# Attention and feed-forward on one core: dummy matmuls ahead of all, alternating row halves for the turned scores, row maxima as two bfloat16 parts

## The chip, the core and the metric

The kernel runs on one core of a Trainium2 chip. The metric is the device time in microseconds (us) of one execution. The kernel before takes 789.25 us (median of 3 runs, 789.15 to 789.5). The engines are named as in the profile: PE is the matmul engine TensorE (PEld its weight loads), DVE the vector engine, ACT the scalar engine, POOL GpSimd, SP the engine that issues nearly all transfers (DMA).

## The reference

An attention over keys and values pooled 8 to 1, then a layer norm and a feed-forward with a residual. The output must be this:

```python
k_p = k.reshape(B, H, Sp, pool, D).mean(axis=3)          # B = H = 8, S = 576, D = 64, Sp = 72
v_p = v.reshape(B, H, Sp, pool, D).mean(axis=3)
scores = scale * np.matmul(q, k_p.transpose(0, 1, 3, 2))
scores = scores - np.max(scores, axis=-1, keepdims=True)
attn = np.exp(scores)
attn = attn / (np.sum(attn, axis=-1, keepdims=True) + 1e-09)
x = np.matmul(attn, v_p)                                 # heads side by side: (B, S, 512)
xn = (x - mu) / np.sqrt(var + 1e-06) * g_ln
out = x + np.maximum(xn @ w_ch1, 0.0) @ w_ch2            # 512 -> 2048 -> 512
```

## The kernel before

The 4608 tokens are 36 tiles `t` of 128 tokens, four to a chunk `c` of 512. The attention of a tile is `scores(t)` (PE, then row maxima `mx` on DVE), the exponentials, and `values(t)` (PE, then the layer norm's sums on DVE). The feed-forward of a chunk is `ffn_in` and `ffn_out` (L1116, L1319) for the first two chunks and a seven-product scheme (`product`, L1160, and `out_seven`, L1277) for the rest. Both weight matrices are split into high and low float16 parts on the chip: `convert` (ACT L535 and L539, DVE L527 and L543) puts a float32 together out of the loaded halves, and `split_w` (ACT L483, then DVE L490 for W1; ACT L483 and L485, then POOL L487 for W2) splits it. Block b's parts lie where block b-1's float32 was, so that the split of b waits for the split of b-1.

The first chunk is special. The exponentials of tiles 0 to 3 are made turned, with the keys on the partitions. `scores(t)` leaves the tile's queries and `mx` in `E[t]`. `probs_turned(t, i)`, with i = 0 for the even heads and i = 1 for the odd ones, multiplies the pooled keys with the queries once more, four heads into one PSUM tile `ps_f` (L849, rows 0 to 63 of the array for i = 0 and rows 64 to 127 for i = 1), and then adds the negative row maxima to the same four results by four float32 matmuls against a negative identity `minus` (L854). ACT takes the exponential (L864) and its float16 part (L865), POOL the remainder (L867). There are three buffers of `ps_f` in this stage, and one of `ps_m`.

The order of all steps is a table of tokens written by hand. `START` covers the first chunks, `STEADY` the rest; a token calls the next step of a generator, so that the order of the tokens is the order on every engine. `LN.2` loads the tokens of batch 0's values, `V0` pools them by five float32 matmuls against a band matrix (L723), `K0` sums the first keys (DVE L1389), `A.t` is the scores of tile t, `E.t.i` the turned exponentials, `B.t` the values, `C.m.b` the conversion and `S.m.b` the split of a weight block, `M1.0` the maximum over W1's first half, `F` and `G` the feed-forward. Engines take their instructions in that order and wait where an input is missing. For `A.t`, DVE reduces the maxima at L800. `M1.0` issues eight dummy matmuls (L463) and the third turned layer norm twelve (L877), each 512 columns of the bfloat16 identity `ident` with no reader.

Of the kernel before, what the change touches and what calls it, by code (L numbers as in the profile page):

```python
# [8 lines left out]
F32 = mybir.dt.float32  # L9
F16 = mybir.dt.float16  # L10
BF16 = mybir.dt.bfloat16
# [3 lines left out]
ALU = mybir.AluOpType  # L15
# [3 lines left out]
P = 128  # L19
B, H, S, D = 8, 8, 576, 64  # L20
POOL = 8
KV = S // POOL
# [6 lines left out]
CH = 512  # L29
# [4 lines left out]
NKT = DM // P  # L34
NFT = FF // P
NPAIR = H // 2
# [21 lines left out]
WARM_MAX = 8  # L58
MAXM = {1: "dve", 2: "act"}
# [5 lines left out]
LN.2 LN.2 LK.0 LK.1 Q.0 K0 R.1.0 Q.1 R.1.1 R.1.2 R.1.3 A.0 Q.1 R.1.3 K0 LK.0 V0 R.1.2 A.0 A.0 A.0 LK.1 HV.1.0 LG R.1.1  # L65
# [309 lines left out]
def attn_ffn_kernel(ctx: ExitStack, tc: tile.TileContext, qT, kT, v, kvn, kvt, g, w1, w2, out):  # L375
    nc = tc.nc
# [103 lines left out]

    def split(src, scale, hi, lo, pool=False):

        nc.scalar.activation(out=hi, in_=src, func=AF.Copy, scale=scale)  # L483
        if pool:
            nc.scalar.activation(out=src, in_=src, func=AF.Copy, scale=scale)  # L485
            yield
            nc.gpsimd.tensor_tensor(out=lo, in0=src, in1=hi, op=ALU.subtract)  # L487
            return
        yield
        nc.vector.scalar_tensor_tensor(  # L490
            out=lo, in0=src, scalar=scale, in1=hi, op0=ALU.mult, op1=ALU.subtract
        )
# [268 lines left out]
    q_sb, E, PT, X, Z, zTs = {}, {}, {}, {}, {}, {}  # L761
# [19 lines left out]
    def scores(t):  # L781
# [19 lines left out]
        if t < TPC:  # L801
            E[t] = q, mx
            return
# [35 lines left out]
    def probs_turned(t, i):  # L839
        q, mx = E[t]  # L840
        mx = mx.rearrange("p a h -> p (a h)")
        if t not in PT:
            PT[t] = wk2.tile([P, 2 * H, P], F16, name="pt")
        pt = PT[t]
        et = phl[t % 2].rearrange("p a h k -> p (a h k)").bitcast(F32).rearrange("p (h c) -> p h c", h=H)
        ps = psum["ps_f"].tile([P, CH], F32, name="ps_f")[:KV].rearrange("p (h c) -> p h c", c=P)
        d = slice(i * D, (i + 1) * D)
        for n in range(NPAIR):
            nc.tensor.matmul(  # L849
                ps[:, n], lhsT=kblk[0][d, n, :], rhs=q[d, n], start=n == 0, stop=False, skip_group_check=True  # L850
            )
        for n in range(NPAIR):
            s = NPAIR * i + n
            nc.tensor.matmul(  # L854
                ps[:, n],
                lhsT=mx[:, s : s + 1].broadcast_to([P, KV]),
                rhs=minus,
                start=False,
                stop=n == NPAIR - 1,
                skip_group_check=True,  # L860
            )
# [531 lines left out]
    def in_tile(c, f, h=None):  # L1393
# [3 lines left out]
        "LK": load_first_k, "LG": load_g, "Q": load_q, "K0": first_k, "V0": lambda: pool_tokens_v(0), "LN": load_tokens, "D": spread_v,  # L1397
# [65 lines left out]
```

## Time and profile before

| | |
|---|---|
| median of 3 runs | 789.25 us |
| span of the profiled execution | 789.2 us |
| PE busy | 772.6 us (98%) |
| PEld busy | 593.2 us (75%) |
| DVE busy | 626.3 us (79%) |
| ACT busy | 469.6 us (60%) |
| POOL busy | 486.9 us (62%) |

The span is the profiled execution's own time; times in rows count from its start. In a row of the timeline stand the start, the time from the start of the first to the end of the last instruction of a group, and in brackets how long the engine had been idle before it and who released it. Instructions overlap in their last part, so that the distance of two starts says what an instruction costs the next one. A float32 matmul stands in the records as two passes: "x8" is four matmuls.

### The profile page before, as it was taken

What the parts mean: (1) busy time and instruction counts of PE and PEld (TensorE: products, weight loads), DVE (VectorE), ACT (ScalarE), POOL (GpSimd) and SP (SyncE); (2) the same over time, 40 slices, a digit from 0 to 9 for tenths busy, and PEclk for the clock granted to TensorE, in tenths of its full rate; (3) what the DMA queues carried; (4) which work ended last, traced back from release to release, by engine and by line L of the source; (5) the groups of instructions that cost most, each with busy time, mean ns of one, the idle gap of its engine ahead of it and who ended that gap; (6) DMA issues with size and microseconds to landing.
All of it is one profiled execution on the core that took longest, in us unless ns stands there. A gap on an engine that the chain in (4) does not pass through costs nothing.

```text
span 789.2 us, 18979 instructions
## 1 busy us (share of the span) xinstructions
PE 772.6 (98%) x7458; PEld 593.2 (75%) x7458; DVE 626.3 (79%) x1296; ACT 469.6 (60%) x880; POOL 486.9 (62%) x597
## 2 busy tenths in 40 slices
PE   6999999999999999999999999999999999999998
PEld 3777444444458665788888888888888888888887
DVE  4998977787669898988789889996797768876554
ACT  3999883233316545577567665756576568555551
POOL 1786468746357766867645683776367638573553
PEclk9999999999999999999999999999999999999999
DMA  8968964631257788968867969578748666664243
GB/s 352 297 208 228 225 166 106 173 98 44 49 135 164 168 201 189 235 180 228 199 172 204 229 163 268 132 219 189 230 83 209 171 165 161 174 148 147 72 130 134
DMA packets 181513, 139.01 MB, mean 176 GB/s; under 512 B 143792, under 2 KB 151600, under 8 KB 179248
## 3 DMA queue, kind: packets, MB, share of 16 engines
q1 hardware_dynamic: 180272, 136.91, 65.2%
q8 instruction: 58, 0.95, 0.5%
q10 hardware_dynamic: 1152, 0.90, 0.4%
q14 instruction: 31, 0.25, 0.1%
HBM read 89.13 MB, written 16.78 MB: 134 GB/s over the span
## 4 chain that ended last, share of the span: by engine, by line
PE 81%; DVE 6%; ACT 6%; POOL 3%; DMA 2%; issue 1%; SPq 0%; POOLq 0%; DVEq 0%; ACTq 0%
PE ps_f L1160 29%; PE ps_f L1277 25%; PE ps_f L1319 14%; PE ps_f L1116 8%; PE ps_a L790 2%; PE ps_a L932 1%; DMA zts<-hl 1%; PE ps_a L933 1%; PE ps_m L723 1%; DVE w L1198 1%; POOL w L487 1%; DVE x L1294 1%; DMA w<-in_kvn_dram 1%; DMA ring<-w2s 1%; ACT w L483 1%
## 5 line engine op out<-in xcount | busy, mean ns | idle before, releaser
L1277 PE MATMUL ps_f<-ring,w 128*128 128x256 f16 x2016 | 231.8, 273 | 1.1 <-DVE x L1294 0.5
L1277 PEld LDWEIGHTS <-w 128*128 128x128 f16 x2016 | 196.1, 98 | 25.6 <-issue 2.0
L1160 PE MATMUL ps_f<-zts,w 128*128 128x256 f16 x1680 | 207.2, 273 | 0.4 <-ACT raw L1179 0.2
L1160 PEld LDWEIGHTS <-w 128*128 128x128 f16 x1680 | 162.9, 98 | 20.4 <-issue 0.8
L1319 PE MATMUL ps_f<-w,ring 128*128 128x512 f16 x576 | 126.8, 379 | 1.3 <-POOL w L487 1.3
L1319 PEld LDWEIGHTS <-ring 128*128 128x128 f16 x576 | 55.9, 98 | 67.1 <-issue 1.6
L1179 ACT COPY raw<-ps_f 128x256 f32<-128x256 f32 x160 | 56.0, 372 | 79.7 <-PE ps_f L1160 69.4
L1160 PE MATMUL ps_f<-zts,tsp 128*128 128x256 f16 x672 | 92.4, 273 | 1.3 <-ACT raw L1179 1.3
L1116 PE MATMUL ps_f<-zts,w 128*128 128x512 f16 (+1 forms) x480 | 85.9, 336 | 1.0 <-DVE ring L1127 1.0
L1196 ACT CAST w<-w 128x512 f16<-128x512 f32 x96 | 59.1, 619 | 38.2 <-POOL w L1219 20.3
L1198 POOL TENSOR_TENSOR w<-w 128x512 f16<-128x512 f32 x48 | 56.8, 1184 | 30.9 <-ACT w L1196 30.8
L1116 PEld LDWEIGHTS <-w 128*128 128x128 f16 x480 | 46.1, 98 | 36.6 <-issue 1.9
L1160 PEld LDWEIGHTS <-tsp 128*128 128x128 f16 x672 | 64.4, 98 | 10.2 <-issue 1.9
L1294 DVE SCALAR_TENSOR_TENSOR x<-ps_f,y,x 128x256 f32<-128x256 f32 (+1 forms) x84 | 42.3, 517 | 34.4 <-PE ps_f L1277 33.5
L826 POOL TENSOR_TENSOR phl<-e,phl 128x512 f16<-128x512 f32 x32 | 39.3, 1227 | 42.4 <-ACT phl L816 34.4
L1215 POOL TENSOR_TENSOR w<-raw 128x256 f32<-128x256 f32 x32 | 24.6, 768 | 56.4 <-ACT raw L1207 38.1
L1085 POOL TENSOR_TENSOR hl<-raw,hl 128x640 f16<-128x640 f32 x28 | 41.9, 1500 | 22.3 <-ACT hl L1083 22.3
L1294 DVE SCALAR_TENSOR_TENSOR x<-ps_f,cy,x 128x256 f32<-128x256 f32 (+1 forms) x84 | 42.2, 515 | 12.8 <-PE ps_f L1277 11.3
L1198 DVE TENSOR_TENSOR w<-raw,w 128x512 f16<-128x512 f32 (+1 forms) x64 | 44.6, 701 | 4.5 <-ACT w L1196 4.2
L1179 ACT COPY phl<-ps_f 128x256 f32<-128x256 f32 x64 | 23.1, 370 | 34.4 <-PE ps_f L1160 33.0
L1174 DVE TENSOR_TENSOR raw<-ps_f,raw 128x256 f32<-128x256 f32 x80 | 32.5, 416 | 9.5 <-PE ps_f L1160 7.5
L1198 DVE TENSOR_TENSOR w<-w 128x512 f16<-128x512 f32 x48 | 36.8, 766 | 4.2 <-ACT w L1196 4.1
(181 smaller groups left out, 1406.8 us busy)
## 6 DMA issues: line engine op xcount, KB each, us to landing
ring<-w2s SPq DMA_DIRECT2D x84, 512.0 KB
q<-in_qT_dram SPq DMA_DIRECT2D x36, 256.0 KB
out_dram<-x SPq DMA_DIRECT2D x34, 256.0 KB
tsp<-in_w_dram SPq DMA_DIRECT2D x8, 1024.0 KB
vr<-in_v_dram SPq DMA_DIRECT2D x56, 144.0 KB
kr<-in_kT_dram SPq DMA_DIRECT2D x28, 288.0 KB
raw<-in_w_dram SPq DMA_DIRECT2D x6, 1024.0 KB
w2s<-phl SPq DMA_DIRECT2D x32, 128.0 KB
```

The lines of the kernel that those rows point to most:

```text
L826: nc.gpsimd.tensor_tensor(out=ph[:, 0, :, KA:P], in0=e[:, :, 0:KA], in1=ph[:, 0, :, 0:KA], op=ALU.subtract)
L1085: nc.gpsimd.tensor_tensor(out=zhl[:, 1, :], in0=src, in1=zhl[:, 0, :], op=ALU.subtract)
L1116: nc.tensor.matmul(ps, lhsT=w[:, part, fs], rhs=zT[:, kz, cols], start=(n == 0), stop=(n == 3 * NKT - 1),)
L1160: nc.tensor.matmul(ps, lhsT=w[:, part, f * P : (f + 1) * P], rhs=z, start=m in (1, 2, 4, 5) and n == 0, stop=m in (2, 3, 4, 7) and n == 3 ...
L1174: nc.vector.tensor_tensor(out=o, in0=ps, in1=o, op=ALU.add)
L1179: nc.scalar.copy(out=o, in_=ps)
L1196: nc.scalar.copy(out=hi, in_=src)
L1198: engine.tensor_tensor(out=lo, in0=src, in1=hi, op=ALU.subtract)
L1215: nc.gpsimd.tensor_tensor(out=s_tmp[:, 0], in0=r01, in1=r11, op=ALU.add)
L1277: nc.tensor.matmul(ps, lhsT=wt[2][:, left, part, f * HC + u * P : f * HC + (u + 1) * P], rhs=b[:, f // FPB, wp, f % FPB], start=n < 4 and ...
L1294: nc.vector.scalar_tensor_tensor(out=x, in0=ps, scalar=scale, in1=x, op0=ALU.mult, op1=ALU.add)
L1319: nc.tensor.matmul(ps, lhsT=h[:, part, i, cols], rhs=w[:, wp, j], start=(n == 0), stop=(n == 3 * NFT // 2 - 1),)
```

## The change

One token `WU` stands ahead of the table: `warm_up` issues ten dummy matmuls of the kind of L463 into the buffer of `ps_m` that `V0` then writes. `scores(t)` for tiles 0 to 3 turns `mx` into `mb`, two bfloat16 parts of the negative maxima, by two DVE operations on 128x8 elements. `probs_turned(t, 0)` now makes the matmuls of both halves, with two `ps_f` tiles at a time: first the eight score matmuls, even and odd heads in turn, then for each half eight bfloat16 matmuls of `mb` against `ident`, two a head in place of one float32 matmul. `probs_turned(t, 1)` keeps its ACT and POOL steps alone.

```diff
+WARM_START = 10
 START = """
-LN.2 LN.2 LK.0 LK.1 Q.0 K0 ...
+WU LN.2 LN.2 LK.0 LK.1 Q.0 K0 ...
...
+    def warm_up():
+        ps = psum["ps_m"].tile([P, CH], F32, name="ps_m").rearrange("p (k c) -> p k c", k=NKT)
+        for _ in range(WARM_START):
+            nc.tensor.matmul(
+                ps, lhsT=ident, rhs=ident.unsqueeze(1).broadcast_to([P, NKT, P]), start=True, stop=True
+            )
...
         nc.vector.tensor_reduce(out=mx, in_=sc, axis=AX.X, op=ALU.max)
         if t < TPC:
-            E[t] = q, mx
+            mx = mx.rearrange("p a h -> p (a h)")
+            mb = small.tile([P, 2, H], BF16, name="mb")
+            nc.vector.tensor_scalar_mul(out=mb[:, 0], in0=mx, scalar1=-1.0)
+            nc.vector.scalar_tensor_tensor(
+                out=mb[:, 1], in0=mx, scalar=-1.0, in1=mb[:, 0], op0=ALU.mult, op1=ALU.subtract
+            )
+            E[t] = q, mb
             return
...
     def probs_turned(t, i):
-        q, mx = E[t]
-        mx = mx.rearrange("p a h -> p (a h)")
         if t not in PT:
             PT[t] = wk2.tile([P, 2 * H, P], F16, name="pt")
-        pt = PT[t]
+            q, mb = E[t]
+            TS[t] = [
+                psum["ps_f"].tile([P, CH], F32, name="ps_f")[:KV].rearrange("p (h c) -> p h c", c=P)
+                for _ in range(2)
+            ]
+            for n in range(NPAIR):
+                for j, ps in enumerate(TS[t]):
+                    d = slice(j * D, (j + 1) * D)
+                    nc.tensor.matmul(
+                        ps[:, n], lhsT=kblk[0][d, n, :], rhs=q[d, n], start=n == 0, stop=False, skip_group_check=True
+                    )
+            for j, ps in enumerate(TS[t]):
+                for n in range(NPAIR):
+                    for part in range(2):
+                        s = NPAIR * j + n
+                        nc.tensor.matmul(
+                            ps[:, n],
+                            lhsT=mb[:, part, s : s + 1].broadcast_to([P, KV]),
+                            rhs=ident,
+                            start=False,
+                            stop=n == NPAIR - 1 and part == 1,
+                            skip_group_check=True,
+                        )
+        pt, ps = PT[t], TS[t][i]
...
-        ps = psum["ps_f"].tile([P, CH], F32, name="ps_f")[:KV].rearrange("p (h c) -> p h c", c=P)
-        d = slice(i * D, (i + 1) * D)
-        for n in range(NPAIR):
-            nc.tensor.matmul(
-                ps[:, n], lhsT=kblk[0][d, n, :], rhs=q[d, n], start=n == 0, stop=False, skip_group_check=True
-            )
-        for n in range(NPAIR):
-            s = NPAIR * i + n
-            nc.tensor.matmul(
-                ps[:, n],
-                lhsT=mx[:, s : s + 1].broadcast_to([P, KV]),
-                rhs=minus,
-                start=False,
-                stop=n == NPAIR - 1,
-                skip_group_check=True,
-            )
         yield
```

On PE, behind the pooling of the values and the scores of tile 0, this is what stood in a row before: the turned scores of the even heads, their maxima, the small matmul of the values' maximum (L470), the odd heads, and the scores of tile 1.

```order
L723 MATMUL ps_m<-w_90,zts 72x512 x5
L790 MATMUL ps_a<-kblk_113,q 64x72 x16
L849 MATMUL ps_f<-q,kblk_113 72x128 x4
L854 MATMUL ps_f<-zts,mx 72x128 x4
L470 LDWEIGHTS rowmax
L470 MATMUL ps_m<-ident,rowmax 128x72
L849 MATMUL ps_f<-q,kblk_113 72x128 x4
L854 MATMUL ps_f<-zts,mx 72x128 x4
L790 MATMUL ps_a<-kblk_113,q 64x72 x16
```

And now, at the same place of PE (lines are 8 to 17 higher): the last of the dummies, the pooling, the scores, and the eight score matmuls of both halves together with the first two of sixteen weight loads and matmuls of `mb`.

```order
L485 LDWEIGHTS ident
L485 MATMUL ps_m<-ident 128x512
L731 MATMUL ps_m<-w_90,zts 72x512 x5
L798 MATMUL ps_a<-kblk_113,q 64x72 x16
L864 MATMUL ps_f<-q,kblk_113 72x128 x8
L871 LDWEIGHTS mb
L871 MATMUL ps_f<-ident,mb 72x128
L871 LDWEIGHTS mb
L871 MATMUL ps_f<-ident,mb 72x128
```

The odd heads have moved ahead of L470, and the scores of tile 1 follow directly behind it. On DVE, this is the beginning of the program before, from the sums of the first keys to the first conversion of weights.

```order
L1389 TENSOR_REDUCE kblk_113<-w_91 128x144 x2
L800 TENSOR_REDUCE mx<-ps_a 128x8
L675 TENSOR_REDUCE mv<-vp 72x1
L438 TENSOR_SCALAR rowmax<-mv 72x1
L439 TENSOR_SCALAR rowmax<-rowmax 72x1
```

And the same place of DVE now: two operations are new behind the maxima, and so behind each of the first four `L800`.

```order
L1408 TENSOR_REDUCE kblk_113<-w_91 128x144 x2
L808 TENSOR_REDUCE mx<-ps_a 128x8
L812 TENSOR_SCALAR mb<-mx 128x8
L813 SCALAR_TENSOR_TENSOR mb<-mx,mb 128x8
L683 TENSOR_REDUCE mv<-vp 72x1
L439 TENSOR_SCALAR rowmax<-mv 72x1
L440 TENSOR_SCALAR rowmax<-rowmax 72x1
```

Nothing else moved on DVE, and on ACT, POOL and SP the order is the same as before.

## Rows read from the trace of the kernel before

**Rows 1.** Waits of PE from 82 us on: us in total, times, longest

```profile
PE ps_f L1160 <- ACT raw L1179: 1.6, 4, 0.6
```

**Rows 2.** The chain that ended last: start, us, what

```profile
79.61 2.15 POOL w L487
```

**Rows 3.** Busy time by stretch: PE, PEld, DVE, ACT, POOL, granted clock, DMA

```profile
13.70:38.90 25.20, 24.56 (x325) 19.87 (x324) 23.27 (x42) 22.77 (x29) 15.72 (x18) 1.00 0.93 329
38.90:81.80 42.90, 39.64 (x465) 30.22 (x465) 37.72 (x78) 41.03 (x64) 32.38 (x40) 1.00 0.77 213
```

**Rows 4.** PE groups, from 6.5 to 9 us and from 12.1 to 13.7 us

```profile
L723 PE MATMUL ps_m<-w,zts 128*72 128x512 f32 x3 | 2.8, 1070 | 6.6 <-DMA w<-in_kvn_dram 6.6
...
L723 PE MATMUL ps_m<-w,zts 128*72 128x512 f32 (+1 forms) x4 | 2.1, 619 | 0.0
```

**Rows 5.** Timeline of PE

```profile
6.56 7.24 PE L723 MATMUL ps_m<-w,zts 128*72 128x512 f32 x10 [6.56 <-DMA w<-in_kvn_dram]
13.73 0.73 PE L790 MATMUL ps_a<-kblk,q 64*64 64x72 f32 x32
14.39 1.09 PE L849 MATMUL ps_f<-q,kblk 64*72 64x128 f32 x8
15.41 1.09 PE L854 MATMUL ps_f<-zts,mx 128*72 128x128 f32 x8
...
39.19 1.13 PE L881 MATMUL ps_m<-zts,x 128*128 128x128 f32 x8 [0.24 <-ACT w L483]
...
42.61 2.75 PE L877 MATMUL ps_m<-ident 128*128 128x512 bf16 x12 [0.70 <-ACT z L902]
45.20 1.05 PE L881 MATMUL ps_m<-zts,x 128*128 128x128 f32 x8
...
81.80 1.24 PE L1319 MATMUL ps_f<-w,ring 128*128 128x512 f16 x5 [1.33 <-POOL w L487]
```

**Rows 6.** Timeline of DVE

```profile
1.51 0.30 DVE L408 CAST ident<-zts 128x128 bf16<-128x128 f32 x1 [1.51 <-POOL zts masks.py:199]
...
9.18 2.77 DVE L1389 TENSOR_REDUCE kblk<-w 128x144 f32<-128x1152 f32 x2 [7.23 <-DMA w<-in_kT_dram]
14.53 0.76 DVE L800 TENSOR_REDUCE mx<-ps_a 128x8 f32<-128x576 f32 x1 [2.58 <-PE ps_a L790]
15.21 0.67 DVE L675 TENSOR_REDUCE mv<-vp 72x1 f32<-72x512 f32 x1
...
17.29 1.21 DVE L543 SCALAR_TENSOR_TENSOR w<-w,tsp 128x1024 int32<-128x1024 int32 x1
...
19.32 0.76 DVE L800 TENSOR_REDUCE mx<-ps_a 128x8 f32<-128x576 f32 x1 [0.17 <-PE ps_a L790]
...
27.47 0.29 DVE L478 TENSOR_REDUCE allmax<-ps_m 128x1 f32<-128x128 f32 x1 [0.35 <-PE ps_m L470]
...
28.35 0.21 DVE L940 TENSOR_SCALAR sm<-ps_a,cv 128x8 f32<-128x8 f32 x1
28.60 0.20 DVE L948 RECIPROCAL rs<-sm 128x8 f32<-128x8 f32 x1
...
35.49 2.46 DVE L490 SCALAR_TENSOR_TENSOR w<-w,gs 128x1024 f16<-128x1024 f32 x1
```

**Rows 7.** Timeline of ACT

```profile
14.32 1.14 ACT L535 ACTIVATE w<-tsp 128x1024 f32<-128x1024 f32 x1
15.36 1.14 ACT L539 ACTIVATE tsp<-tsp 128x1024 int32<-128x1024 uint16 x1
...
18.87 0.72 ACT L483 ACTIVATE vh<-vp,sv 72x512 f16<-72x512 f32 x1 [1.08 <-DVE sv L445]
...
37.98 1.15 ACT L483 ACTIVATE w<-w,gs 128x1024 f16<-128x1024 f32 x1 [0.51 <-DVE w L490]
...
41.30 0.68 ACT L899 ACTIVATE zts<-ps_m,cv 128x512 f16<-128x512 f32 x1
```

**Rows 8.** Waits of SP, 6 to 28 us: us in total, times, longest

```profile
SPq L510 <- DMA tsp<-in_w_dram: 2.1, 1, 2.1
```

**Rows 9.** Timeline of SP and of POOL

```profile
13.69 0.33 SPq L510 DMA_DIRECT2D raw<-in_w_dram  x1
...
35.70 3.25 POOL L867 TENSOR_TENSOR pt<-phl,pt 72x512 f16<-72x512 f32 x2
```

**Rows 10.** Line L490: duration ns min/median/max, first and last start

```profile
L490 DVE SCALAR_TENSOR_TENSOR w<-w,gs x8: 1272/1277/2456, 30.4 to 100.0; 128x1024 f16<-128x1024 f32 x8
```

More of the change, by code (lines that the diff above doesn't have):

```diff
@@ L64 @@
 START = """
-LN.2 LN.2 LK.0 LK.1 Q.0 K0 R.1.0 Q.1 R.1.1 R.1.2 R.1.3 A.0 Q.1 R.1.3 K0 LK.0 V0 R.1.2 A.0 A.0 A.0 LK.1 HV.1.0 LG R.1.1
+WU LN.2 LN.2 LK.0 LK.1 Q.0 K0 R.1.0 Q.1 R.1.1 R.1.2 R.1.3 A.0 Q.1 R.1.3 K0 LK.0 V0 R.1.2 A.0 A.0 A.0 LK.1 HV.1.0 LG R.1.1
 V0 R.2.0 LG V0 C.1.0 C.1.0 C.1.0 C.1.0 R.2.0 E.0.0 E.0.0 E.0.0 V0 E.0.1 A.1 V0 V0 A.1 A.1 E.1.0 K0 V0 E.0.0 V0 V0 Q.0
@@ L758, in spread_v @@
             queue.dma_start(out=VB[b][KV + i * KR : KV + (i + 1) * KR], in_=vh[KA:])
-    q_sb, E, PT, X, Z, zTs = {}, {}, {}, {}, {}, {}
+    q_sb, E, PT, X, Z, zTs, TS = {}, {}, {}, {}, {}, {}, {}
     def segments(t):
@@ L1396, in attn_ffn_kernel @@
     ops = {
-        "LK": load_first_k, "LG": load_g, "Q": load_q, "K0": first_k, "V0": lambda: pool_tokens_v(0), "LN": load_tokens, "D": spread_v,
+        "WU": warm_up, "LK": load_first_k, "LG": load_g, "Q": load_q, "K0": first_k, "V0": lambda: pool_tokens_v(0), "LN": load_tokens, "D": spread_v,
         "KN": lambda: pool_tokens_k(1), "VN": lambda: pool_tokens_v(1), "R": load_raw, "A": stage_a,
```

## The prediction

> **What bounds the kernel now.** I read the waits of PE first, because PE is busy for 98% of the span. From 82 us to the end PE waits for 4 us in all: five rows, the largest of which is the one shown [rows 1]. So behind that point the end moves only as PE's own work or its start moves, and the change touches none of that work. The chain that ended last says what starts it: POOL's last remainder of the second weights, 79.61 plus 2.15 [rows 2], for which PE waits 1.33 us before it goes on with the feed-forward's first output at 81.80 [rows 5]. The question is how much earlier that remainder comes. In the busy times by stretch [rows 3], DVE works 23.27 of the 25.2 us from 13.7 to 38.9, and its first 0.8 us are a wait for PE; ACT works 41.03 of the 42.9 us from there to 81.8. PE is as full as they are (24.56 of 25.2), but fullness alone doesn't make it the bound: the timelines show who waits for whom. DVE waits for PE at 14.53 for 2.58 us, at 19.32 for 0.17 and at 27.47 for 0.35 [rows 6]; ACT waits for DVE at 18.87 and at 37.98 [rows 7]. The path therefore is: first keys and first pooling, DVE nearly without a break from 14.53 to 37.9, ACT behind it to 79.5, POOL, PE. I work out the shift of that path, place by place; a minus is earlier.
>
> **The dummies and the pooling.** `ident` is ready at 1.51 + 0.30 = 1.81 [rows 6]. At full clock a 512-column dummy costs (45.20 - 42.61)/12 = 0.216 us [rows 5], at half the clock 0.43, so ten end by 6.1 at the latest, ahead of 6.56, where the pooling starts on its landing [rows 5]. They cost nothing there; were the cover gone, they would cost at most what lies behind 6.56, and it is nothing. In exchange the pooling finds a warm engine: its first passes took 1070 ns, the last four 619 ns with 2.1 us for all four [rows 4], the lower level of 1.2 GHz and the full one of 2.4 (the column of granted clock has no record that early, so the durations decide). Ten passes at 2.1/4 = 0.52 end at 6.56 + 5.2 = 11.8, where they ended at 13.73. If the clock doesn't rise in time the gain shrinks to zero, and no reason makes it a loss.
>
> **What is late next** is the key sum on DVE: 9.18 + 2.77 = 11.95, started by a landing [rows 6]. The scores of tile 0 need its second half: half of 0.73 [rows 5], plus 0.07 on either side (13.73 + 0.73 to 14.53), so `mx` of tile 0 starts at 12.46 and not at 14.53: **-2.05**. The bounds of this term are 0 and -2.05.
>
> **The turned scores.** Before, a half costs 15.41 - 14.39 = 1.02 for the scores and as much for the maxima [rows 5], 4.1 us a tile, 16.4 us for four tiles. Now eight matmuls on alternating row halves cost between 1.02 (pairs run side by side) and 2.04 (they don't). L790 alternates rows and columns already, and takes 0.73 for 32 passes where L849 takes 1.09 for 8; I take 1.1. Sixteen bfloat16 matmuls of 128 columns cost at least a quarter of 0.216 each, 0.9 us, and with a load before each that nothing hides some three times that; I take 1.1. PE is rid of 1.4 to 2.2 us a tile. **None of it is on the path**: ACT has no wait for these matmuls in the rows that matter [rows 7], and DVE's 0.17 and 0.35 are all that it can get. What PE saves turns into PE's idle time.
>
> **The two small operations.** They are added to DVE, which is on the path. The next operation starts 0.68 after `mx` does today (14.53 to 15.21), while the first of the new two must wait for its end at 0.76, some 0.1 more. No row shows the two themselves; the nearest are L940 and L948, 128x8 too, 0.25 from start to start [rows 6]. So a pair costs 0.1 + 0.25 + 0.08 (the next overlaps as L675 does `mx`) = 0.43; the bounds are 0.3 and 0.6. Four pairs would be 1.7.
>
> **The sum along the path.** -2.05 at `mx` of tile 0, +0.43 for its pair: -1.62. Then DVE's L543 at 17.29 needs ACT's L539. ACT's L535 can't start ahead of its weights, which land at 13.69 (the issue of SP that waited for that landing [rows 8, 9]); 14.32 becomes 13.7, so L539 ends 0.62 earlier, at 15.88, and L543 goes to 15.92: **-1.37**. The wait of 0.17 goes: -1.54; second pair: **-1.11**. Third pair: it fits into the 0.35 that DVE waits for PE at 27.47 and the 0.08 of overlap; ACT and POOL, which feed PE there, are 1.2 earlier, so PE isn't late: -1.11 stays. Fourth pair: **-0.68**. With that DVE's split at 35.49 and ACT's wait for it at 37.98 are 0.68 earlier [rows 6, 7], ACT goes on without a break, and the last remainder, PE at 81.80 and the end follow. The front of the transfers needs no more than before: the same bytes in the same order.
>
> One wait is new: with three `ps_f` buffers and two taken a tile, tile 1's second score matmul waits for ACT's exponential of tile 0's even heads. Queued behind it on PE are the values of tile 0, the scores of tile 2, the eight dummies. They wait for POOL's remainder of tile 0's odd heads anyhow, which is later on ACT and POOL than that exponential; cost nothing, and if that cover were gone at most the 0.6 of the exponential.
>
> The profiled span is 789.2, the median 789.25; I take the sum off the latter: 789.25 - 0.7 = **788.5**.
>
> **The rivals.** *Faster: DVE and POOL collide less.* The split at 35.49 takes 2.46 us where its line's median is 1.28 [rows 6, 10], and POOL's two remainders beside it take 3.25 [rows 9]. POOL is about 1.2 earlier in the new order and DVE 0.7, so the two may meet for less long. At the most 1.18 is won: -1.86; ACT's own limit there is -1.37 and its wait of 0.51, -1.88. That gives 789.25 - 1.87 = 787.4. Against it: POOL's work there is one block without a break, longer than the shift between the two. The Trainium skill, page "GPSIMD Engine Reference", section "Specifications", says that GpSimd's way to SBUF is shared with VectorE and contended when a vector instruction has two SBUF inputs; the split has two. By that rule the operations that overlap are slow whatever the order, and the sum would stay at 788.5; the rows agree that an overlap is dear, and don't show how long it would be now.
>
> *Slower: PE goes cold.* What PE saves opens one long gap. Before L881 at 39.19 PE waits 0.24 [rows 5]; the operand is made by DVE and so comes 0.7 earlier, at 38.5. PE's work ahead of it ends with tile 3's maxima: their pair stands one L543 ahead of the split, so it is done at 35.49 - 0.68 - 1.2 = 33.6, and 1.1 us of matmuls later PE has nothing left: idle from 34.7 to 38.5, 3.8 us, where the longest wait behind the start is now 1.33 [rows 5]. The one long wait in the trace, the 6.56 us of the start, was followed by the lower level [rows 4]. The page "TensorE: Matmul & The Clock Gate" of the Trainium skill, section "HAM oscillation — how this bites in real kernels", says the same of waits between bursts: the engine falls back to the half clock and begins the next burst slow. By that rule this rival is the forecast. From rows: from L881 at 39.19 to ACT's use of the result at 41.30 [rows 5, 7] lie 2.1 us, of which some 1.8 would double, and ACT is without a break there, so the path loses about 1.75; the twelve dummies would cost up to 2.6 more, of which I let 1 reach ACT. That is -0.7 + 1.75 to -0.7 + 2.75: 790.3 to 791.3, say 790.9. It decides from the point where the gap is long enough to lose the clock, which no row shows; the other gaps that open are shorter.
>
> *No gain: the dummies don't bring the clock up in time,* or a pair costs 0.6. Each takes away 0.7 or more; 789.25. That the alternating halves don't overlap is no rival in time: PE has the room.
>
> **How the numbers follow.** The forecast (787.8 to 789.0) 0.48; no gain (789.0 to 789.9) 0.15; the faster rival (786.9 to 787.6) 0.25; the slower one (790.3 to 791.3) 0.12. A measurement of this kernel tells 0.2%, 1.6 us, from no change: 787.7 and 790.8 are the borders. Faster is the faster rival, 0.25; slower is three quarters of the slower one, 0.09; the rest is the same, 0.66. The range takes in the faster rival and the beginning of the slower one: 786.9 to 790.4.
>
> **What would show it.** In the profile of the changed kernel: dummies from 1.9 to 6.1 at most; passes of the pooling of 0.6 us from the first or second on; `mx` of tile 0 at 12.5; the new pair 0.4 long; DVE's next maxima 1.5, 1.1, 1.1 and 0.7 earlier; a tile's turned scores in 2.2 us; ACT's wait for the split near 37.3; PE idle before L881 for 3.5 to 4 us, and that matmul as long as now. Wrong would make it: scores of tile 0 at 13.7, a split at 35 of 1.3 us, passes of L881 that are twice as long, or a PE that waits behind 82 us for something that it doesn't wait for now.

## The result, and the profile of the changed kernel

The changed kernel takes 794.04 us (median of 5, 793.69 to 795.29), beside it the kernel before 789.5 (789.15 to 790.95): 1.0052 times as long, 95% interval 1.0041 to 1.0063. The forecast was 788.5 and no measurable change; it is 4.5 us slower. Lines of the new kernel are 1 to 19 higher: `mx` L808, the pair L812 and L813, conversion L535, L543, L547 and L551, split L491 and L498, W2's remainder L495, maximum L471 and L479 with its eight dummies L464, turned scores L864, their maxima L871, exponentials L883 and L884, POOL's remainder L886, turned layer norm L896, L900 and L908, values L947 to L949, layer norm's sums L959, `ffn_out` L1338.

The chain that ended last still runs through POOL's last remainder of the second weights [rows 2], now at 83.21, so 3.60 later:

```profile
83.21 2.15 POOL w L495
```

The rest, 0.8 us of the 4.4 between the two spans (793.6 and 789.2), arises behind 85 us, most of it in PE's waits for single landings (0.4 us for `pt`, 0.2 more for `ring`). So the answer lies ahead of 83 us. The busy times of the same two stretches [rows 3], and of two shorter ones in them (columns: PE, PEld, DVE, ACT, POOL, then granted clock, share and rate of the transfers):

```profile
13.70:38.90 25.20, 18.17 (x268) 13.00 (x265) 22.67 (x43) 20.26 (x27) 14.51 (x20) 0.86 0.96 338
38.90:81.80 42.90, 39.87 (x454) 31.04 (x455) 35.47 (x69) 38.59 (x59) 27.29 (x35) 0.92 0.69 197
...
22.40:29.20 6.80, 6.35 (x64) 3.63 (x62) 4.93 (x14) 4.54 (x7) 5.51 (x10) 0.50 1.01 343
39.45:46.30 6.85, 5.27 (x35) 3.89 (x36) 4.23 (x9) 4.87 (x8) 2.63 (x3) 0.50 0.35 89
```

PE's busy time in the first stretch fell from 24.56 to 18.17 us, as the change wants. But the granted clock, 1.00 in both stretches before, is 0.86 and 0.92: from 22.4 to 29.2 and from 39.45 to 46.3 it is 0.50, the lower of its two levels. Ahead of each PE had been waiting (the second begins within PE's wait from 38.49 to 40.99). PE's waits from 13.7 to 47 us, in the kernel before and in the changed one (us in total, times, longest):

```profile
PE ps_m L877 <- ACT z L902: 0.7, 1, 0.7
PE ps_a L929 <- POOL pt L867: 0.6, 1, 0.6
PE ps_m L881 <- ACT w L483: 0.2, 1, 0.2
```

```profile
PE ps_f L871 <- DVE mb L812: 3.2, 2, 2.0
PE ps_m L900 <- ACT w L491: 2.5, 1, 2.5
PE ps_a L947 <- ACT pt L884: 1.4, 1, 1.4
PE ps_a L948 <- POOL pt L886: 1.2, 1, 1.2
PE ps_a L798 <- DMA q<-in_qT_dram: 0.5, 1, 0.5
PE ps_f L864 <- ACT phl L883: 0.3, 1, 0.3
```

1.5 us of waiting became 9.1. Where they fall, and what came behind them, on PE's timeline [rows 5]:

```profile
1.88 4.01 PE L485 MATMUL ps_m<-ident 128*128 128x512 bf16 x10 [1.88 <-DVE ident L409]
6.53 4.63 PE L731 MATMUL ps_m<-w,zts 128*72 128x512 f32 x10 [0.64 <-DMA w<-in_kvn_dram]
...
17.92 1.23 PE L871 MATMUL ps_f<-ident,mb 128*72 128x128 bf16 x16 [1.20 <-DVE mb L812]
...
20.67 0.20 PE L947 MATMUL ps_a<-vh,pt 72*128 72x65 f16 x1 [1.43 <-ACT pt L884]
22.06 0.20 PE L948 MATMUL ps_a<-vh,pt 72*128 72x65 f16 x1 [1.19 <-POOL pt L886]
...
24.74 3.60 PE L464 MATMUL ps_m<-ident 128*128 128x512 bf16 x8
...
37.27 1.23 PE L871 MATMUL ps_f<-ident,mb 128*72 128x128 bf16 x16 [2.03 <-DVE mb L812]
40.99 2.05 PE L900 MATMUL ps_m<-zts,x 128*128 128x128 f32 x8 [2.50 <-ACT w L491]
```

The dummies and the warm pooling came as forecast. The eight dummies L464 take 3.60 where they took 1.90 at full clock in the kernel before, the first matmuls of the second turned layer norm 2.05 instead of 1.13 [rows 5]. The eight dummies before:

```profile
25.47 1.90 PE L463 MATMUL ps_m<-ident 128*128 128x512 bf16 x8
```

DVE's timeline of the changed kernel [rows 6]:

```profile
11.89 0.76 DVE L808 TENSOR_REDUCE mx<-ps_a 128x8 f32<-128x576 f32 x1 [0.74 <-PE ps_a L798]
12.68 0.17 DVE L812 TENSOR_SCALAR mb<-mx 128x8 bf16<-128x8 f32 x1
12.88 0.17 DVE L813 SCALAR_TENSOR_TENSOR mb<-mx,mb 128x8 bf16<-128x8 f32 x1
...
22.81 1.22 DVE L535 TENSOR_REDUCE wm<-ring 128x1 f32<-128x1024 f32 x1 [0.70 <-DMA ring<-in_w_dram]
...
25.17 0.75 DVE L808 TENSOR_REDUCE mx<-ps_a 128x8 f32<-128x576 f32 x1
25.95 0.28 DVE L812 TENSOR_SCALAR mb<-mx 128x8 bf16<-128x8 f32 x1
26.26 1.07 DVE L813 SCALAR_TENSOR_TENSOR mb<-mx,mb 128x8 bf16<-128x8 f32 x1
28.48 0.29 DVE L479 TENSOR_REDUCE allmax<-ps_m 128x1 f32<-128x128 f32 x1 [1.15 <-PE ps_m L471]
...
32.88 2.18 DVE L551 SCALAR_TENSOR_TENSOR w<-w,ring 128x1024 int32<-128x1024 int32 x1
...
36.42 0.80 DVE L812 TENSOR_SCALAR mb<-mx 128x8 bf16<-128x8 f32 x1
...
38.47 1.28 DVE L498 SCALAR_TENSOR_TENSOR w<-w,gs 128x1024 f16<-128x1024 f32 x1
...
46.11 0.23 DVE L959 TENSOR_SCALAR sm<-ps_a,cv 128x8 f32<-128x8 f32 x1 [2.49 <-PE ps_a L949]
```

And POOL's remainders beside the pairs [rows 9]:

```profile
25.04 2.28 POOL L886 TENSOR_TENSOR pt<-phl,pt 72x512 f16<-72x512 f32 x2 [0.58 <-ACT pt L884]
32.20 3.87 POOL L886 TENSOR_TENSOR pt<-phl,pt 72x512 f16<-72x512 f32 x2 [1.54 <-ACT pt L884]
36.03 1.15 POOL L923 TENSOR_TENSOR zts<-z,zts 128x512 f16<-128x512 f32 x1
```

The first pair takes 0.17 and 0.17 us. The third's second operation takes 1.07 and ends at 27.33, where POOL's two remainders end (27.32); the fourth's first takes 0.80 and ends at 37.22, where POOL's next subtraction ends (37.18). POOL's block at 32.20 has also moved from one large operation of DVE to another: the conversion ahead of the fourth maxima takes 2.18 (1.34 before), while the split at 38.47 is back at 1.28 (2.46 before). Two suspects, then: the **clock**, lost in PE's new gaps, and the **pair**, stretched beside POOL.

The way of the delay stands in one table, which also holds the experiments. Each column is an operation of DVE, the last one POOL's last remainder: its start in the profiled execution of that kernel minus its start in that of the kernel before (first line, us). "Split done" is the first operation behind the split at 35.49 [rows 6], "behind PE" the same operation one tile later, which needs PE's next values, "V" the maximum of the second block of values.

| kernel | ratio to before, 95% | clock at 0.5 (us) | mx 1 | mx 2 | allmax | mx 3 | split done | behind PE | V | last |
|---|---|---|---|---|---|---|---|---|---|---|
| before | 1 | none | 19.32 | 26.37 | 27.47 | 33.69 | 37.87 | 41.95 | 66.27 | 79.61 |
| changed | 1.0052 (1.0041-1.0063) | 22.4-29.2, 39.5-46.3 | -2.41 | -1.21 | +1.01 | +1.95 | +1.80 | +4.16 | +4.07 | +3.61 |
| e1 dummies ahead | 0.9989 (0.9980-0.9998) | 24.9-28.3 | -1.93 | -1.02 | +0.19 | +0.17 | +0.65 | +0.65 | +0.71 | +0.63 |
| e2 and pair | 1.0039 (1.0026-1.0051) | 40.6-44.0 | -1.55 | -0.62 | +0.66 | +0.58 | +1.54 | +3.13 | +3.30 | +2.99 |
| e5 and halves in turn | 1.0037 (1.0025-1.0049) | 38.6-45.4 | -2.24 | -0.92 | -1.06 | -0.70 | +0.04 | +2.39 | +4.38 | +3.89 |
| e3 one maximum | 1.0034 (1.0021-1.0046) | 18.9-25.8, 36.0-42.8, 70.1-73.6 | -2.02 | -1.17 | -0.23 | -0.05 | +0.68 | +2.11 | +4.28 | +4.32 |
| e4 clock kept | 1.0037 (1.0023-1.0050) | none | -2.19 | -1.29 | +0.04 | -0.23 | +0.86 | +0.85 | +2.25 | +1.76 |
| e11 kept, first gap | 1.0063 (1.0050-1.0076) | 36.6-43.4 | -2.24 | -1.33 | 0.00 | -0.30 | +0.67 | +2.40 | +3.86 | +3.39 |
| e12 kept, second gap | 1.0053 (1.0033-1.0072) | 18.6-28.8, 629.6-633.0 | -1.74 | -0.93 | +1.39 | +1.97 | +1.82 | +1.82 | +1.86 | +1.87 |
| e7 one part, no pair | 1.0038 (1.0025-1.0052) | 20.7-27.6, 37.8-44.6 | -2.32 | -1.50 | +0.45 | +0.88 | +0.45 | +2.81 | +2.86 | +2.40 |
| e8 and clock kept | 1.0013 (1.0004-1.0021) | none | -2.35 | -1.19 | -1.32 | -0.77 | -0.02 | -0.03 | +0.80 | +0.52 |
| e9 and POOL 4 later | 1.0016 (1.0000-1.0033) | 42.9-46.3, 70.2-73.6 | -1.80 | -0.57 | -0.74 | -0.64 | -1.76 | -1.29 | +3.89 | +3.97 |
| e13 and POOL 2 later | 0.9989 (0.9977-1.0000) | none | -2.28 | -1.52 | -1.65 | -0.73 | -1.01 | -1.02 | -0.29 | -0.76 |
| e6 dummies, clock kept | 0.9991 (0.9983-1.0000) | none | -2.16 | -1.35 | -1.65 | -1.91 | -3.03 | -2.13 | -2.24 | -2.24 |
| e10 and POOL 4 later | 0.9992 (0.9981-1.0004) | none | -2.46 | -1.12 | -1.14 | -0.91 | -2.09 | -1.62 | -1.48 | -1.66 |
| e15 and POOL 2 later | 0.9985 (0.9976-0.9994) | none | -2.03 | -1.02 | -1.38 | -0.54 | -0.82 | -0.82 | -0.68 | -0.82 |
| e14 = e4, POOL 2 later | 1.0038 (1.0026-1.0050) | none | -2.27 | -1.08 | -0.03 | -0.31 | +0.67 | +0.66 | +1.91 | +1.45 |
| e16 = e4, POOL 4 later | 1.0066 (1.0049-1.0083) | 37.7-41.1 | -2.19 | -1.26 | +0.06 | -0.24 | +1.90 | +3.15 | +4.76 | +4.28 |

In the changed kernel the front is 2.4 us early at `mx` of tile 1; landings take half of it (DVE waits 0.70 for `ring` at 22.81, PE 0.45 for `q` at 23.57); at `allmax` it is 1.0 late, and behind PE's second gap 4.2. The low stretch at the end of every kernel, about 3 us at most, is left out of the table.

### The profile page after: what moved, and what is told of

Read it like the earlier page. It is cut to its first block, busy times and chain, and to the rows that moved or that the text cites. A ratio compares the mean times of both kernels' runs of the same rounds, so it can differ in the third digit from the quotient of the medians.

```text
span 793.6 us, 19007 instructions
## 1 busy us (share of the span) xinstructions
PE 772.8 (97%) x7468; PEld 590.8 (74%) x7468; DVE 628.8 (79%) x1304; ACT 469.8 (59%) x880; POOL 483.3 (61%) x597
## 4 chain that ended last, share of the span: by engine, by line
PE 81%; DMA 6%; DVE 5%; ACT 3%; POOL 2%; issue 1%; SPq 1%; POOLq 0%; ACTq 0%; DVEq 0%
PE ps_f L1179 28%; PE ps_f L1296 25%; PE ps_f L1338 14%; PE ps_f L1135 9%; PE ps_a L798 2%; DMA q<-in_qT_dram 2%; PE ps_a L951 1%; DMA zts<-hl 1%; PE ps_a L952 1%; DMA vr<-in_v_dram 1%; DVE w L1217 1%; DMA w<-in_kT_dram 1%; POOL w L495 1%; DMA pt<-phl 1%; DVE x L1313 1%
## 5 line engine op out<-in xcount | busy, mean ns | idle before, releaser
L1338 PE MATMUL ps_f<-w,ring 128*128 128x512 f16 x576 | 126.8, 379 | 1.4 <-POOL w L495 1.4
L1338 PEld LDWEIGHTS <-ring 128*128 128x128 f16 x576 | 55.9, 98 | 67.2 <-issue 1.6
L840 POOL TENSOR_TENSOR phl<-e,phl 128x512 f16<-128x512 f32 x32 | 39.2, 1226 | 42.5 <-ACT phl L830 42.4
```

The lines of the kernel that those rows point to most:

```text
L840: nc.gpsimd.tensor_tensor(out=ph[:, 0, :, KA:P], in0=e[:, :, 0:KA], in1=ph[:, 0, :, 0:KA], op=ALU.subtract)
L1338: nc.tensor.matmul(ps, lhsT=h[:, part, i, cols], rhs=w[:, wp, j], start=(n == 0), stop=(n == 3 * NFT // 2 - 1),)
```

## The experiments

Each kernel ran beside the kernel before on the same chip; the ratios are those of the table. The kernel before took 790.05 to 790.57 us there. Line numbers differ from kernel to kernel; the names of the tiles tell the operations.

### The parts alone: e1, e2, e5, e3

e1 is the kernel before with the token `WU` and `warm_up`. e2 adds the pair with no reader, e5 the order of the matmuls:

```diff
 # e2, in scores(t)
+            mf = mx.rearrange("p a h -> p (a h)")
+            mb = small.tile([P, 2, H], BF16, name="mb")
+            nc.vector.tensor_scalar_mul(out=mb[:, 0], in0=mf, scalar1=-1.0)
+            nc.vector.scalar_tensor_tensor(out=mb[:, 1], in0=mf, scalar=-1.0, in1=mb[:, 0], ...)
             E[t] = q, mx
 # e5, the changed kernel in probs_turned(t, 0), no pair
-                    for part in range(2):
-                        ... lhsT=mb[:, part, s : s + 1], rhs=ident
+                    ... lhsT=mx[:, s : s + 1], rhs=minus
 # e3: e5 with
-                for n in range(NPAIR):
+                for n in range(NPAIR - 1, NPAIR):
```

> Only the ten dummy matmuls ahead of all; the turned scores, their float32 maxima and the work of DVE stay as before. Clock theory (the loss comes from PE's idle stretches, in which the granted clock falls to its low level): PE keeps its 4.1 us a tile of turned scores, so the clock stays full from 5.5 us on, mx of tiles 0 and 1 start 2.6 and 2.4 us earlier than before, the landings of ring at 22.8 and of q at 23.5 leave about 1.2 of it, and the time is 787.5 to 788.5. Pair theory (the two operations of mb on DVE are the price): the same, since the pair isn't there. Order theory (an earlier front only runs into landings and collisions, and is worth nothing or less): 789.2 to 790.5.

> The dummies ahead of all, and the two operations of mb on DVE behind each of the first four maxima, with no reader; the matmuls stay as before (float32 maxima, halves apart). Pair theory: most of the loss is here, 2 us or more over the kernel with the dummies alone, 790 to 792. Clock theory: PE is as full as in that kernel, the clock stays full, and the pairs cost what DVE spends on them, 0.4 for each, or up to 1.3 where POOL works beside: 0.3 to 1.3 us in all, 788 to 789.5.

> Dummies ahead and the halves in turn, but the maxima stay float32, one matmul a head, and no pair on DVE: PE has about 1 us a tile less to do than before (the halves run side by side), half of what the whole change takes away. Clock theory: idle stretches half as long; the granted clock falls in at least one place between 22 and 47 us, as it did in the kernel with the dummies alone (24.9 to 28.3), and the time is 0 to 2.5 us over the kernel before. Pair theory: without the pair 1 to 1.5 us under the kernel before.

> Alternating halves and dummies as in the changed kernel, but no pair on DVE, and of each half's four maxima one float32 matmul only (the other three heads go without their maximum): PE has some 1.7 us a tile less to do than in the kernel with the dummies alone, about as little as the changed kernel or a little less, DVE has nothing to do more. Clock theory: PE idles as in the changed kernel, the granted clock falls to 0.5 once or twice between 22 and 47 us, and the time is 791 to 794 in spite of the missing pairs. Pair theory: 787 to 788.5.

**Measured.** e1 0.9989, a gain of 0.9 us, at the edge of what can be told, and a little less than expected (787.5 to 788.5, for a kernel before at 789.5; it took 790.47 here). Even it lost the clock, from 24.9 to 28.3, behind waits of 0.95 and 0.52 us. Of its eleven executions the three with a mean clock of 0.997 or 0.998 took 789.89, 790.65 and 791.24, the other eight 788.34 to 790.27. e2 is 3.2 us over the kernel before and 4.1 over e1: what the pair theory expected (2 us or more over e1), and more than its range. But its trace shows the clock too: DVE's split came late, PE waited 2.54 us for it, and the clock fell from 40.6 to 44.0; between "split done" and "behind PE" that costs 1.6. e5 and e3 have no pair and are 3.3 and 2.6 us over the kernel before: the clock theory's numbers, e5 above its range. In e5:

```profile
39.23 2.04 PE L894 MATMUL ps_m<-zts,x 128*128 128x128 f32 x8 [3.48 <-ACT w L491]
```

the wait of 3.48 is the gap, the matmuls behind it take 2.04 us where they took 1.13, and the path loses 2.35 us there (+0.04 to +2.39). Neither theory alone holds: each part without the other brings a loss of the same size, by another way.

### The clock kept: e4, e11, e12

Dummy matmuls of the kind of L464 stand in PE's gaps, written into the buffer that the next real matmuls fill:

```diff
-KEEP_BUSY = {2: 12}
+KEEP_BUSY = {1: 11, 2: 12}
+KEEP_T = {1: 8, 3: 9}      # ahead of the turned scores of tiles 1 and 3
+KEEP_V = {0: 14}           # ahead of the values of tile 0
 # e11: KEEP_T = {1: 8}, KEEP_V = {0: 14}, KEEP_BUSY as before; e12: KEEP_T = {3: 9}, KEEP_BUSY = {1: 11, 2: 12}
```

> The changed kernel with 42 more dummy matmuls where its PE waits: 8 ahead of the turned scores of tile 1 and 14 ahead of the values of tile 0 (first stretch of low clock), 9 ahead of the turned scores of tile 3 and 11 ahead of the second turned layer norm (second stretch). Clock theory: the granted clock stays full through, the eight dummies of the weights' maximum take 1.9 us again instead of 3.6 and the first matmuls of the second turned layer norm 1.1 instead of 2.05, and the time comes to 789 to 790.5, 3.5 to 5 less than the changed kernel. Pair theory: the pairs are still there, 792.5 to 794.

> The changed kernel with dummies in its first stretch of low clock only (8 ahead of the turned scores of tile 1, 14 ahead of the values of tile 0). Clock theory: full clock until some 38 us, then one low stretch ahead of the second turned layer norm, which costs the 1.5 to 2.4 us that it cost in the changed kernel (from the end of the split to the next use of PE's result); the time is between that of the changed kernel and that with all gaps filled, 2.5 to 4 us over the kernel before, most of the loss still there, since that stretch is the dearer one.

> The changed kernel with dummies in its second stretch only (9 ahead of the turned scores of tile 3, 11 ahead of the second turned layer norm). Clock theory: low clock from 22 to 29 us alone, which makes the eight dummies of the weights' maximum last 3.6 us and DVE wait for their result, 1 us at the most; the time is near that with all gaps filled, 2.3 to 3.3 us over the kernel before.

**Measured.** e4 has no low stretch, and all its executions have a mean clock of 0.999 or 1.000. Its PE:

```profile
24.02 1.90 PE L466 MATMUL ps_m<-ident 128*128 128x512 bf16 x8
...
39.96 1.16 PE L908 MATMUL ps_m<-zts,x 128*128 128x128 f32 x8
```

Both prices are gone, `allmax` comes at +0.04 instead of +1.01, and "behind PE" nothing is added (+0.86 to +0.85, where the changed kernel goes from +1.80 to +4.16). The time falls to 1.0037, by 1.2 us (the two intervals still overlap): a quarter to a third of what the clock theory expected, and 792.88 us lies in the pair theory's range. So the clock is at most a part of the loss. e11 and e12 remove the delay where they should (e11: `allmax` 0.00, then +1.73 in the second gap; e12: `allmax` +1.39, then nothing in the second gap), but neither can be told from the changed kernel (1.0063 and 1.0053, their intervals overlap its own); by the medians they are 4.9 and 3.6 us over the kernel before, both above their ranges. A price for each gap in the time cannot be read from them; behind 60 us other waits come in (below).

### The pair taken out: e7, e8

The maxima go straight into one bfloat16 number a head (they are rounded), with one bfloat16 matmul a head; e8 has the dummies of e4 as well, 5 for 8 ahead of tile 1.

```diff
-        mx = scalar_tile("mx", H)
+        mx = small.tile([P, H], BF16, name="mb") if t < TPC else scalar_tile("mx", H)
...
-            nc.vector.tensor_scalar_mul(out=mb[:, 0], ...)
-            nc.vector.scalar_tensor_tensor(out=mb[:, 1], ...)
...
+                    ... lhsT=mx[:, s : s + 1], rhs=minus_b      # negative bfloat16 identity
```

> The changed kernel without the pair: DVE's maxima of the first four tiles go straight into one bfloat16 number a head, with no further operation, and one bfloat16 matmul a head against a negative identity takes the place of two (the maxima are rounded; a softmax doesn't need them exact). PE has still less to do than in the changed kernel, DVE as much as before. Clock theory alone: low clock in two stretches as in the changed kernel, 2.5 to 4.5 us over the kernel before. Pair theory alone: 1 to 1.5 us under it. Both prices: between 1 and 3 us over it, the changed kernel's loss less that of the pair.

> The same with 39 more dummy matmuls in PE's gaps (5 ahead of the turned scores of tile 1, 14 ahead of the values of tile 0, 9 ahead of the turned scores of tile 3, 11 ahead of the second turned layer norm): neither the pair nor the low clock. If these two are the whole loss: clock 1.000 and 1 to 1.8 us under the kernel before, no better than the dummies ahead with a kept clock, since PE's savings are not on the path. If the new order itself costs (the second score matmuls wait for ACT, values come later): no change or slower than before.

**Measured.** e7 1.0038 with both low stretches: 2.2 us over the kernel before by the medians, which is the case of both prices, and 3.0 by the ratio, which the clock theory alone would allow too. Keeping the clock in it brings 2.0 us (e8, 1.0013, intervals apart, though two of its eleven executions still had a clock of 0.998 and 0.997). And e8 against e4, which differ by the pair and its matmuls: 1.9 us, intervals apart. So the pair is dear, where the forecast had 4 times 0.43 with the third hidden. But e8 is still slower than before, and 1.7 us slower than e1 with a kept clock (e6 below): something third is left.

### DVE and POOL: e6, e9, e10, e13, e15, e14, e16

In e8's trace the third cause stands on DVE behind the fourth maxima, with POOL beside it:

```profile
33.58 2.25 DVE L555 SCALAR_TENSOR_TENSOR w<-w,ring 128x1024 int32<-128x1024 int32 x1
35.75 2.17 DVE L502 SCALAR_TENSOR_TENSOR w<-w,gs 128x1024 f16<-128x1024 f32 x1
```

```profile
32.47 2.28 POOL L890 TENSOR_TENSOR pt<-phl,pt 72x512 f16<-72x512 f32 x2
34.71 2.13 POOL L927 TENSOR_TENSOR zts<-z,zts 128x512 f16<-128x512 f32 x1
```

Before, DVE's conversion was first, ahead of POOL at 35.70, and only the split was stretched (2.46) [rows 6, 9]:

```profile
34.35 1.21 DVE L543 SCALAR_TENSOR_TENSOR w<-w,ring 128x1024 int32<-128x1024 int32 x1
```

Now POOL is 3.2 us earlier and DVE 0.8, so POOL is first, and both operations are stretched. In the changed kernel and in every run with the pair these two operations run free (1.22 to 1.28 us each): there the fourth pair stands in the same place and meets POOL instead. e6 is e1 with 6 dummies ahead of the values of tile 0. The others hold POOL back by memsets (0.56 us each) ahead of its remainders for tile 2, 4 or 2 of them:

```diff
         yield
+        for _ in range(POOL_LATE.get((t, i), 0)):          # POOL_LATE = {(2, 0): 4} or {(2, 0): 2}
+            nc.gpsimd.memset(pt[:KV, H + 4 * i : H + 4 * i + 4], 0.0)
         nc.gpsimd.tensor_tensor(
```

e9 and e13 are e8 with 4 and 2, e10 and e15 are e6 with 4 and 2, e16 and e14 are e4 with 4 and 2.

> The dummies ahead of all, and six more dummy matmuls ahead of the values of tile 0, where PE waits for POOL's remainder; nothing else. The kernel with the dummies ahead alone lost the clock from 24.9 to 28.3 in its profiled execution, and its executions with a clock below 0.999 took 1.4 us longer than those with 1.000. Clock theory: clock 1.000 in every execution, 1.2 to 1.8 us under the kernel before. If the clock is not what makes those executions longer: 0.9 us under it, as there.

> The kernel with one bfloat16 part and the kept clock, and four more memsets on POOL (about 0.55 us each, an estimate from the 0.36 of 128x320) ahead of its remainders for tile 2. In that kernel POOL reaches them at 32.5, ahead of DVE's conversion of the weights (33.6) and split (35.8), and both take 2.2 us beside them instead of 1.2 and 1.3; in the kernel with the dummies ahead and a kept clock DVE was first (32.4 against 33.8), and its two took 1.2 and 1.3. Phase theory (what is left of the loss is that POOL gets ahead of DVE and meets it twice): with POOL some 2.2 us later the conversion takes 1.2 us, and the time is 1 to 2 us less than without the memsets. If the phase is not the cause: no change, or a little more.

> The kernel with the dummies ahead of all and a kept clock, and the same four memsets. Phase theory: this kernel's executions lie between 788.0 and 790.8, as DVE or POOL is first there; with POOL later DVE is always first, and they stay near 788 to 789, 1.5 to 2.2 us under the kernel before. If the phase is not the cause: as without the memsets, 0.7 us under the kernel before.

> One bfloat16 part, kept clock, and two memsets of 0.56 us ahead of POOL's remainders for tile 2 instead of four. Phase theory: the conversion of the weights behind the fourth maxima takes 1.2 us where it took 2.25, the clock stays full, and the time is 0.5 to 1.5 us under the kernel before (it was 1.0 over it). If the phase is not the cause: 0.8 to 1.5 us over it, as without the memsets.

> Dummies ahead of all, kept clock, and the two memsets; the turned scores as before. Phase theory: DVE is first there in most executions already; 0.7 to 1.7 us under the kernel before. Otherwise: 0.7 under it.

> The changed kernel with the kept clock, pairs and all, and the same two memsets. In the kernel without them the fourth pair took 1.14 and 1.02 us beside POOL's remainders. Phase theory: with POOL 1.1 us later the pair takes its 0.17 and 0.17, and the time falls by 0.8 to 2 us, to 0.4 to 1.6 us over the kernel before (it was 2.4 to 2.9). If the pair costs by itself, not by POOL: no change.

> The changed kernel with the kept clock, pairs and all, and four memsets ahead of POOL's remainders for tile 2: these then start at about 35.0, behind the fourth pair (34.1). If the pair is dear only beside POOL: the fourth pair takes 0.17 and 0.17, the conversion behind it starts 1.7 us earlier than with two memsets, and in executions with a full clock the time falls by 1 to 2 us, to about 1 to 2 us over the kernel before. If the pair is dear by itself: it takes 1 and 1 us again, 3 us over the kernel before. As with one part and four memsets, PE may find a gap at 42 us in which the clock falls, in some executions.

**Measured.** In e9's trace the conversion takes 1.21 and the split 1.34, and "split done" goes from -0.02 to -1.76; but POOL came so late that PE waited 2.03 us for ACT at 42.5 and lost the clock. Its executions fall apart: the five with a full clock took 789.28 to 790.59, the seven with 0.998 and less 791.61 to 795.92. With two memsets (e13) no such gap shows in the profiled execution:

```profile
33.62 1.21 DVE L556 SCALAR_TENSOR_TENSOR w<-w,ring 128x1024 int32<-128x1024 int32 x1
34.75 2.18 DVE L503 SCALAR_TENSOR_TENSOR w<-w,gs 128x1024 f16<-128x1024 f32 x1
```

and the time is 0.9989, 1.9 us under e8, intervals apart, inside what the phase theory expected; two of its twelve executions had a clock of 0.998 and 0.997 and took 791.93 and 792.47, the others 787.85 to 790.66. In the traces 1.0 of it stands at "split done" and 1.3 at "last"; the rest they don't show. So the third cause is shown: the new order, without the pair and with the clock kept, loses by POOL's being first, and what else it may lose is too small for these times (e13 against e6 and e15). The old order isn't free of it: in e1's profiled execution (790.65 us, its median is 789.56) the two operations take 1.97 and 2.18. e6 shows the other side: its fastest execution, the profiled one (788.02 us), has conversion and split at 1.21 and 1.34. It has no execution with a lost clock, and is yet no faster than e1: the 1.2 to 1.8 us expected of the kept clock didn't come; its executions spread from 788.02 to 790.75 all the same. e10 gained nothing over it, e15 no more than can be told apart: as a cause of that spread the phase is not shown. e15 is the fastest of all medians, 788.91 us, 0.9985 (0.9976 to 0.9994).

e14 and e16 were to free the fourth pair from POOL. e14 didn't: with the pairs, POOL was at its remainders at 32.83 even so, the pair took 1.02 and 1.03, and the time is that of e4. e16 missed by 0.17 us, and shows what a miss is. DVE, and POOL:

```profile
34.22 2.13 DVE L815 TENSOR_SCALAR mb<-mx 128x8 bf16<-128x8 f32 x1
36.39 1.07 DVE L816 SCALAR_TENSOR_TENSOR mb<-mx,mb 128x8 bf16<-128x8 f32 x1
```

```profile
34.05 2.27 POOL L897 TENSOR_TENSOR pt<-phl,pt 72x512 f16<-72x512 f32 x2
36.28 1.16 POOL L934 TENSOR_TENSOR zts<-z,zts 128x512 f16<-128x512 f32 x1
```

POOL begins at 34.05, the pair's first operation at 34.22, and it ends at 36.35, with POOL's two (36.32); the second begins at 36.39, behind POOL's next, and ends at 37.46, with it (37.44). An operation of 0.17 us cost 2.13. The time that was expected did not come (1.0066, with e11 the slowest of all), but the mechanism stands plainer here than in any other run.

The Trainium skill says this on its page "SBUF — State Buffer", section "Who interferes with whom": VectorE and GpSimd share one pair of ports as an exclusive lock, which a VectorE instruction with two SBUF inputs, or one in a two-port mode, needs; the engine that starts first holds it for its whole instruction, and the other stands still. The trace agrees in these four rows, with one difference: the first of the pair stood still through two instructions of POOL in a row (34.05 to 36.32), not one. It agrees also in who is spared: in the changed kernel `mx`, which reads PSUM, takes 0.75 us at 25.17 beside POOL as elsewhere.

## Why the prediction was wrong, step by step

**What failed, in short.** Three steps of the forecast: the price of the pair, 0.43 with the third one hidden (beside POOL it cost 1.35 and 0.97); PE's saved time, which became idle time and was taken to be free (the clock fell to 0.50 twice, 1.2 to 2.0 us of the total); and the meetings of DVE and POOL, which were held at their old size (1.9 us between e8 and e13).

**Right.** Dummies from 1.88 to 5.9, the pooling warm (4.63 us for ten passes where it lasted from 6.56 to 13.73), a tile's turned scores in 1.10 and 1.23 us (forecast 2.2 in all), the first pairs at 0.4, and the statement that PE's saving doesn't reach the end: e13, with all of it and nothing against it, is no faster than e15, with none of it. The front's gain was larger than its bound, -2.64 at the first `mx` for -2.05: the landing behind the key sum, held fixed in the forecast, came 0.8 us earlier. The new wait for ACT's exponential is 0.32 us on PE and cost nothing. Two numbers of the working don't come out, and neither changes the outcome: 12.46 is 2.07 before 14.53, not 2.05, and the lower bound of what PE saves a tile, 1.4, is above what the two upper prices ahead of it would leave. Measured from start to start it is 1.8 (4.1 before, 2.32 from 11.75 to 14.07 now).

**The transfers.** "The front of the transfers needs no more than before" failed: DVE and PE wait for `ring` and `q`, and of -2.41 at `mx` 1 -1.21 is left at `mx` 2. The forecast had -1.11 there: the landings took what the front had gained beyond the forecast, and this step changes no sign.

**The pair.** What failed is its price, 0.43 with bounds of 0.3 and 0.6. It came from rows of 128x8 operations [rows 6] that met no POOL; the split that takes 2.46 beside POOL instead of 1.28 [rows 9, 10] was read as a matter of the split alone. Beside POOL a pair costs what is left of POOL's block: 1.35 and 0.97 in the changed kernel, 3.20 in e16. That the third pair "fits into the 0.35 that DVE waits for PE" failed with it: in e4, with a full clock and PE early, `allmax` still waits for the pair, and -1.29 becomes +0.04. Taking the pair and its matmuls out brings 1.9 us (e4 against e8).

**PE goes cold.** The forecast took what "turns into PE's idle time" to be free. The slower rival had the right mechanism and the right place, though its time, 790.3 to 791.3, was too low as well: a gap ahead of the second turned layer norm, forecast 3.8 us, found as 2.03 and 2.50 with the maxima between; forecast price 1.75 to 2.75, found 2.36 (+1.80 to +4.16). Two things failed. "The other gaps that open are shorter" was taken for harmless, and waits of 1.20, 1.43 and 1.19 us in a row lost the clock as well, with 3.60 us for the eight dummies. And 0.12 was too low a chance: no row of the kernel before spoke against it, and the rows showed the one long wait followed by the lower level [rows 4]. The Trainium skill, page "TensorE: Matmul & The Clock Gate", section "HAM oscillation — how this bites in real kernels", says that waits between bursts bring the next burst at the half clock; the trace agrees (0.50 behind both groups of waits), though the waits of the page's example are longer than those of the changed kernel. What the clock costs of the total, 1.2 us (e4) or 2.0 (e8), is less than the prices at the two places: of the 3.3 us that e4 is ahead of the changed kernel at "behind PE", 1.8 are left at "V".

**DVE and POOL collide.** The faster rival had the mechanism, and the 1.18 that it hoped for came: the split takes 1.28 in the changed kernel. But POOL, whose work follows ACT, was 3.5 us earlier there (32.20 for 35.70) and met the conversion ahead of the fourth maxima (2.18 for 1.34) and the fourth pair (0.97 for 0.4) in its place. The rival asked if DVE and POOL meet for less long, and not what POOL would meet instead. In e8, without the pair, POOL met two operations in place of one; that is the 1.9 us between e8 and e13.

**The sum.** From e13 at 0.9989 it is 0.0024 to e8 (POOL's phase), 0.0024 from there to e4 (the pair), 0.0015 from there to the changed kernel's 1.0052 (the clock). These are the steps of one chain, so they add up whatever the causes, and they are no three shares of the changed kernel. The order of the steps is a choice, the pair takes the very block of POOL that the conversion and the split take in e8, and in e2 the pair alone opened the gap that lost the clock. That e13 stands at the forecast's 788.5 (0.9990 of 789.25) is luck: it has no pair, for which the forecast had three times 0.43.

**What stays open.** Between "behind PE" and "V" e5, e3, e4, e11, e9 and e16 lose a further 1.4 to 5.2 us, e14 1.2, e8 and e13 0.8 and 0.7, the changed kernel nothing. In the profile most of it is a wait of POOL for a landing, in e5:

```profile
67.32 0.73 POOL L677 TENSOR_TENSOR vr<-vr 72x256 f32<-72x256 f32 x1 [2.13 <-DMA vr<-in_v_dram]
```

That transfer landed 8.7 us after its issue there, 7.1 in the changed kernel, and no later than 6.6 in the kernel before; why it varies is not settled, nor why e11 and e12, each with one gap filled, are no faster than the changed kernel. Whether a pair free of POOL would cost only its 0.4 us wasn't shown either for the third and the fourth: no run had them free (the first two, which met no POOL, did).

## What to carry to other kernels

Ask of a saving on an engine that isn't the bound where its idle time will lie, and what the engine does next: several waits of one or two microseconds in a row may cost the clock, and then the saved work comes back as slow work on the path. Price a small vector operation by what GpSimd does at that moment, not by its size; a block that comes 0.2 us ahead of it adds the whole block. And where two engines contend, work out which of them gains more from the change, since the one that gets ahead is the one that makes the other wait.

## What was unexpected of the hardware

The clock fell behind waits that were each short: 0.95 and 0.52 us in e1 (full until 24.9), 1.20, 1.43 and 1.19 in the changed kernel, always to 0.50, for 3.4 or 6.8 us or, once, for 10.2. Not every such row of waits did it: 0.75, 0.92, 1.03 and 0.87 us between 17 and 24 us left e5 at 1.00, and what decides is not shown. Contention depended on what POOL ran, as far as one run tells: in e9 DVE's split took 1.34 us beside POOL's memsets, in e8 2.17 beside POOL's subtraction. Eight score matmuls on alternating row halves take 1.10 us where four on one half took 1.09: the pairs run wholly side by side.
